# The last four on-chip transposes of a fused attention and feed-forward kernel go to the DMA, and the loads around them move

## The chip, the core and the metric

The kernel runs on one core of a Trainium2 chip. The metric is the device time of one execution, in microseconds (us): the median of several runs. The engines of the core are named as in the profile: PE (matrix engine; PEld is its weight load), DVE (vector), ACT (scalar), POOL and SP. POOL and SP also issue DMA transfers, each in the order of its own instruction stream.

## The reference

Batch 8, 8 heads, 1024 rows, head size 64. Keys and values are first projected along the rows to 64, then there is an ordinary softmax attention against these 64, and its output goes through a gated feed-forward block of width 1536:

```
k_proj = einsum('ks,bhsd->bhkd', E, k);  v_proj = einsum('ks,bhsd->bhkd', F, v)
scores = matmul(q, k_proj^T) / 8
attn   = exp(scores - max) / (sum + 1e-9)
x      = matmul(attn, v_proj), heads side by side: (8192, 512)
g = x @ w_gate;  out = (g * sigmoid(g) * (x @ w_val)) @ w_out
```

All inputs and the output are float32; the kernel computes in bf16 on PE.

## The kernel before, in words

The work is cut into 16 chunks of 512 rows: batch `b` (0 to 7) and half `ch` (0 or 1), chunk number `c = 2b + ch`. The feed-forward block is the main stream: for each chunk, 12 steps `f`, so 192 steps `t = 12c + f`. A step is four matmuls of 128x512 against `w_gate` (`f_g`, L322), four against `w_val` (`f_v`, L322), and, one chunk late, one or two groups of four against `w_out` (`f_y`, L360). Every third group of a chunk's `f_y` ends a 128-row output tile, which ACT copies out (`ysb`, L370) and SP stores (L372).

The attention of the next batch is written by hand into the gaps of this stream. Slot `2t` lies after `f_g` of step `t`, slot `2t+1` after its `f_v` and `f_y`; `put(slot, function, ...)` places a piece there, and every engine executes its share in this order (nothing is reordered later). In each slot the loads come first. The pieces, with the names used below:

- `load_k`, `load_v`, `load_q`, `load_wo`: DMA transfers issued by POOL, with a cast to bf16. k and v are 1 MB each in bf16 and per batch, a half of q 0.5 MB (one per chunk), a half of the output weights 0.75 MB. At the start of the kernel they are listed one after the other, beside the gate and value weights.
- KV (`u_KV`, L147): the two projections, 8 matmuls each for k and v. KT (`u_KT`, L172): the projected keys turned over and written as the block-diagonal tile `BD`.
- The turn of q, either on PE, T (`u_T`, four pieces per chunk with four transposes each, L193, and a copy by ACT), or by one DMA transpose, TD (`u_TD`, tile `qTd`, L205, issued by SP).
- S (`u_S`, L227): the scores, eight pieces per batch, `u` = 0 to 7 (0 to 3 belong to the first half), four small matmuls each, and the exponential on ACT (`ee`). R (`u_R`): sum and reciprocal on DVE. N (`u_N`, L258): the product of both on POOL, tile `AAd` (or `AA`).
- The turn of the attention weights, either on PE, A (`u_A`, four pieces per chunk with four transposes each, L274, and a copy by DVE), or by one DMA transpose, AD (`u_AD`, tile `AT`, L212, issued by SP). SP's stores of output tiles and its TD and AD stand in one stream.
- PV (`u_PV`, L285): the product with the values, four pieces per chunk, from `AT` to the chunk's input `xT`.

The list `BY_DMA` says which chunks are turned by DMA: before, all of batches 1 to 7 but the first half of batch 1. Batch 0 is always turned on PE. In `place(b)` stand the slots of a batch: `sa` for S, `sp` for PV, and, for batch 1, `tt` and `ta` for T and A. For b of 3 and more, S lies in slots `48(b-1)+6` and every third after it; these are the same before and after.

Of the kernel before, what the change touches and what calls it, by code (L numbers as in the profile page):

```python
# [15 lines left out]
B = 8  # L16
# [11 lines left out]
CH = 2  # L28
CW = 512
NIT = B * CH * NFT  # L30
BY_DMA = [(b, ch) for b in range(1, B) for ch in range(CH)][1:]


@with_exitstack
def kernel(
# [49 lines left out]
    def load_k(b, h0=0, h1=H):  # L85
        if h0 == 0:
            kb[b] = kv_pool.tile([P, H, NJ, D], BF16, name="kb", tag="kb")
        nc.gpsimd.dma_start(
            out=kb[b][:, h0:h1].rearrange("p h j d -> p h (j d)"),
            in_=k[b, h0:h1].rearrange("h (p j) d -> p h (j d)", j=NJ),  # L90
        )
# [10 lines left out]
    def load_q(b, ch, parts=1):  # L102
        t = q_pool.tile([P, H, 4, D], BF16, name="qb", tag="qb")
        qb[b, ch] = t
        n = H // parts
        for i in range(parts):
            nc.gpsimd.dma_start(
                out=t[:, i * n : (i + 1) * n].rearrange("p h j d -> p h (j d)"),
                in_=q[b, i * n : (i + 1) * n].rearrange("h (p c j) d -> p c h (j d)", c=2, j=4)[:, ch],
            )  # L110

    def load_w_gv(c0, c1, which=(0, 1)):
        cs = slice(c0 * P, c1 * P)
        for wsrc, wdst in [((moe_w_gate, wg), (moe_w_val, wv))[i] for i in which]:
            nc.gpsimd.dma_start(
                out=wdst[:, :, cs],
                in_=wsrc[:, cs].rearrange("(t p) c -> p t c", p=P),
            )

    def load_wo(i):  # L120
        nc.gpsimd.dma_start(
            out=wo[:, 6 * i : 6 * (i + 1), :],
            in_=moe_w_out[6 * i * P : 6 * (i + 1) * P, :].rearrange("(t p) c -> p t c", p=P),
        )
# [93 lines left out]
    def u_S(b, u, at="a"):  # L218
        ch, w = divmod(u, 4)
        g, i = divmod(w, 2)  # L220
        ps = bank(at, [P, 4, P], FP32, "sc")
        if (b, ch) in BY_DMA:
            t = qT[b, ch, "d"][:].rearrange("p (h i) t -> p i h t", i=2)[:, i, 4 * g : 4 * g + 4]
# [163 lines left out]
    def put(s, fn, *a):  # L387
        slots[s].append((fn, a))

    def place(b):  # L390
        s0 = 48 * (b - 1)
        if b == 1:
            put(30, u_TD, 1, 1)
            put(34, u_KV, 1, "k")
            put(36, u_KT, 1)
            put(40, u_KV, 1, "v")
            sa = (37, 38, 39, 40, 48, 50, 52, 54)
            tt = (35, 36, 37, 38)
            ta = (41, 42, 43, 44)
            put(57, u_AD, 1, 1)  # L400
            sp = (43, 44, 45, 46, 66, 67, 68, 69)
        else:
            put(s0, u_KV, b)
            put(s0 + 3, u_KT, b)
            o = 14 if b == 2 else 6
            put(s0 + (3 if b == 2 else -6), u_TD, b, 0)
            put(s0 + (5 if b == 2 else -4), u_TD, b, 1)
            sa = [s0 + o + 3 * j for j in range(NJ)]
            put(sa[3] + 4, u_AD, b, 0)
            put(sa[7] + 4, u_AD, b, 1)  # L410
            sp = [s0 + i for i in (39, 41, 43, 45, 57, 59, 61, 63)]
        for j in range(NJ):
            if (b, j // 4) not in BY_DMA:
                put(tt[j], u_T, b, j)
                put(ta[j], u_A, b, j)
            put(sa[j], u_S, b, j)
            put(sa[j] + 1, u_R, b, j)
            put(sa[j] + 1, u_N, b, j)
        for i in range(8):
            put(sp[i], u_PV, b, i // 4, i % 4)  # L420
# [5 lines left out]
    with tc.manual_schedule():  # L426
        load_k(0, 0, 4)
        ef = []
        for which, src in (("E", E), ("F", F)):
            raw = const.tile([KP, S], FP32, name=f"{which}raw")  # L430
            nc.sync.dma_start(out=raw[:], in_=src)
            ef.append(raw)
        zeros = const.tile([P, CW], BF16, name="zeros")
        nc.vector.memset(zeros[:], 0.0)
        make_identity(nc, ident_fp[:])
        make_identity(nc, ident_bf[:])
        for i in range(2):
            nc.vector.memset(BD[i][:], 0.0)
            nc.vector.memset(BDV[i][:], 0.0)

        def turn(which):
            for half in range(2):
                ps = bank("v", [P, 4, KP], FP32, "efp")
                for i in range(4):
                    j = 4 * half + i
                    nc.tensor.transpose(
                        out=ps[:, i, :],
                        in_=ef[which][:, bass.ds(j, P, step=NJ)],
                        identity=ident_fp[:KP, :KP],
                    )  # L450
                js = slice(4 * half, 4 * half + 4)
                copy((nc.scalar, nc.vector)[which], (ET, FT)[which][:, js, :], ps[:])

        def warm(n):

            ps = bank("v", [P, CW], FP32, "warm")
            for _ in range(n):
                nc.tensor.matmul(  # L458
                    out=ps[:], lhsT=zeros[:, 0:P], rhs=zeros[:],
                    start=True, stop=True,  # L460
                )


        load_k(0, 4, 8)
        load_q(0, 0, 2)
        load_v(0, (0, 4, 8))
        load_w_gv(0, 1)
        load_w_gv(1, 2)
        load_w_gv(2, 4)
        warm(8)  # L470
        turn(0)
        turn(1)
        warm(7)
        u_KV(0, "k", (0, 4), at="y")
        warm(2)
        u_KT(0, at="v", prs=(0, 2))
        warm(2)
        u_KV(0, "k", (4, 8), at="y")
        warm(2)
        u_KT(0, at="v", prs=(2, 4))  # L480
        u_T(0, 0, "a", nc.scalar)
        u_T(0, 1, "a", nc.vector)
        u_T(0, 2, "a", nc.scalar)
        u_S(0, 0, "g")
        u_T(0, 3, "v", nc.vector)
        u_S(0, 2, "g")
        u_S(0, 1, "a")
        u_S(0, 3, "a")
        u_R(0, 0)
        u_N(0, 0)  # L490
        u_R(0, 2)
        u_N(0, 2)
        load_w_gv(4, 6, (0,))
        u_KV(0, "v", (0, 4), at="y")
        warm(1)
        u_A(0, 0, nc.scalar)
        u_R(0, 1)
        u_N(0, 1)
        u_R(0, 3)
        u_N(0, 3)  # L500
        u_A(0, 2, nc.scalar)
        u_KV(0, "v", (4, 8), at="y")
        load_w_gv(4, 6, (1,))
        load_q(0, 1)
        load_w_gv(6, 8)
        load_w_gv(8, 10)
        load_w_gv(10, 12)
        load_wo(0)
        load_wo(1)
        load_k(1)  # L510
        warm(1)
        u_PV2(0, 0, 0, 0, nc.scalar)
        u_PV2(0, 0, 1, 0, nc.vector)
        u_A(0, 1, nc.scalar)
        u_A(0, 3, nc.vector)
        f_mm(0, 0, 0, 0)
        f_mm(0, 0, 1, 0)
        u_PV2(0, 0, 0, 1, nc.scalar)
        u_PV2(0, 0, 1, 1, nc.vector)
        f_mm(0, 1, 0, 0)  # L520
        f_mm(0, 1, 1, 0)

        for i, u in enumerate(range(4, 8)):
            put(12 + i, u_T, 0, u)
            put(14 + i, u_S, 0, u)
            put(15 + i, u_R, 0, u)
            put(15 + i, u_N, 0, u)
            put(19 + i, u_A, 0, u, nc.scalar)
        put(21, u_PV, 0, 1, 0)
        put(22, u_PV, 0, 1, 1)  # L530
        put(23, u_PV, 0, 1, 2)
        put(23, u_PV, 0, 1, 3)
        put(20, load_q, 1, 0)
        put(20, load_v, 1)
        put(20, load_q, 1, 1)
        for b in range(1, B):
            place(b)
        for b in range(2, B):
            s0 = 48 * (b - 1) - (12 if b == 2 else 24)
            put(s0, load_k, b)  # L540
            put(s0 + 2, load_v, b)
            put(s0 + 4, load_q, b, 0)
            put(s0 + 6, load_q, b, 1)

        for s in slots:
            slots[s].sort(key=lambda x: x[0] not in (load_k, load_v, load_q))


        ypart = defaultdict(list)
        for c in range(B * CH - 1):  # L550
            for n in range(NFT):
                f = n if c else 4 + (2 * n + 1) // 3
                ypart[(c + 1) * NFT + f].append((c, n))

        for t in range(NIT):
            c, f = divmod(t, NFT)
            i = 1 if t < 2 else None
            f_g(c, f, i)
            run_slot(2 * t)
            f_v(c, f, i)  # L560
            for a in ypart.pop(t, ()):
                f_y(*a)
            run_slot(2 * t + 1)
        for n in range(9):
            f_y(B * CH - 1, n)
        f_y_last(B * CH - 1, 3)
        assert not slots and not ypart
# [29 lines left out]
```

The softmax here doesn't subtract the row's maximum and nothing guards it: scores larger than these inputs give would overflow.

## Time and profile before

| | |
|---|---|
| median of 6 runs | 573.81 us (573.4 to 574.19) |
| time of the profiled execution | 573.73 us |
| its span in the profile | 572.0 us |
| PE busy | 562.4 us, 98% |
| DVE, ACT, POOL busy | 336.7, 236.9, 107.9 us |
| DMA, mean over the span | 107 GB/s |
| granted PE clock | 0.9 of full speed or more in every slice |

The profile times start at the beginning of the span; the 1.73 us between span and time lie around it. Rates of DMA count bytes as they are written, so a load with a cast counts at half of what is read.

### The profile page before, as it was taken

To read this page: it belongs to the slowest core of one execution; us is meant where nothing else is said; L and a number is where in the kernel's file an instruction comes from. 1 tells how busy PE (TensorE), PEld (TensorE's weight loads), DVE (VectorE), ACT (ScalarE), POOL (GpSimd) and SP (SyncE) were. 2 spreads that over 40 slices of the span, in tenths; PEclk is the share of its full clock that TensorE was granted. 3 is DMA by queue.
4 is the path that set the end of the run, shared out by engine and by line. 5 is a ranking of instruction groups with operands and counts; after the bars stand their busy time and mean duration, and the time that the engine had idled before them with its cause. 6 is when DMAs were issued, how large, how long until landed. Compare 5 with 4: busy or idle time off the path is not lost.

```text
span 572.0 us, 7867 instructions
## 1 busy us (share of the span) xinstructions
PE 562.4 (98%) x2910; PEld 268.5 (47%) x2967; DVE 336.7 (59%) x580; ACT 236.9 (41%) x416; POOL 107.9 (19%) x121
## 2 busy tenths in 40 slices
PE   8999999999999999999999999999999999999997
PEld 4654444444444444444444444444444444444444
DVE  2787566666466754666556665567546675554550
ACT  1665444354435434444335434354342543443232
POOL 6724121134002500124001330023200220000000
PEclk9999999999999999999999999999999999999999
DMA  9999993549901697038941499204990124100012
GB/s 168 195 201 206 201 154 76 91 71 195 202 32 46 109 192 153 18 75 128 192 103 38 63 177 198 59 20 92 188 182 36 43 51 74 38 37 27 30 39 92
DMA packets 105927, 61.34 MB, mean 107 GB/s; under 512 B 58016, under 2 KB 97696, under 8 KB 105888
## 3 DMA queue, kind: packets, MB, share of 16 engines
q0 software_dynamic: 42288, 29.89, 36.0%
q1 hardware_dynamic: 63312, 30.68, 25.3%
q8 instruction: 23, 0.38, 0.3%
q10 hardware_dynamic: 288, 0.26, 0.1%
q14 instruction: 16, 0.13, 0.1%
HBM read 60.29 MB, written 16.78 MB: 135 GB/s over the span
## 4 chain that ended last, share of the span: by engine, by line
PE 96%; ACT 1%; DMA 1%; issue 1%; DVE 1%; SPq 0%
PE yps L360 29%; PE vps L322 29%; PE gps L322 29%; PE kvp L147 3%; PE sc L227 3%; PE pv L285 2%; DMA Fraw<-in_F_dram 1%; PE warm L458 1%; PE aTp L274 0%; PE qTp L193 0%; PE kTp L172 0%; ACT xT L135 0%; DVE zz L242 0%; ACT th L334 0%; DVE AA L258 0%
## 5 line engine op out<-in xcount | busy, mean ns | idle before, releaser
L341 DVE SCALAR_TENSOR_TENSOR s<-th,gps 128x512 f32<-128x512 f32 x192 | 130.5, 680 | 138.0 <-ACT th L334 137.8
L322 PE MATMUL gps<-xT,wg 128*128 128x512 bf16 (+1 forms) x755 | 195.7, 377 | 1.2
L322 PE MATMUL vps<-xT,wv 128*128 128x512 bf16 (+1 forms) x761 | 195.9, 377 | 0.8
L360 PE MATMUL yps<-wo,hT 128*128 128x512 bf16 (+2 forms) x761 | 191.5, 376 | 0.8
L334 ACT ACTIVATE th<-gps 128x512 f32<-128x512 f32 x192 | 114.7, 597 | 162.6 <-PE gps L322 155.1
L346 DVE TENSOR_TENSOR hT<-s,vps 128x512 bf16<-128x512 f32 x192 | 132.0, 688 | 22.1 <-PE vps L322 1.5
L360 PEld LDWEIGHTS <-hT 128*128 128x128 bf16 x780 | 76.2, 98 | 89.9
L258 POOL TENSOR_TENSOR AAd<-ee,rr 128x512 bf16<-128x512 f32 x52 | 54.1, 1040 | 319.5 <-issue 168.5
L322 PEld LDWEIGHTS <-wv 128*128 128x128 bf16 x776 | 73.9, 98 | 82.9 <-issue 3.3
L322 PEld LDWEIGHTS <-wg 128*128 128x128 bf16 x776 | 74.0, 98 | 81.3 <-issue 0.6
L370 ACT ACTIVATE ysb<-yps 128x512 f32<-128x512 f32 (+1 forms) x65 | 38.4, 591 | 78.1 <-PE yps L360 74.4
L135 ACT CAST xT<-pv 128x512 bf16<-128x512 f32 x62 | 36.1, 585 | 51.3 <-PE pv L285 50.3
L242 DVE TENSOR_REDUCE zz<-ee 128x8 f32<-128x512 f32 x64 | 43.5, 679 | 17.7 <-ACT ee L231 17.6
L231 ACT ACTIVATE ee<-sc 128x512 f32<-128x512 f32 x64 | 37.8, 595 | 17.4 <-PE sc L227 17.4
L285 PE MATMUL pv<-AT,BDV 128*128 128x512 bf16 x60 | 22.6, 379 | 0.1
L227 PEld LDWEIGHTS <-qTd 128*128 128x128 bf16 x208 | 16.0, 98 | 12.3
L227 PE MATMUL sc<-BD,qTd 128*128 128x128 bf16 x208 | 20.1, 219 | 0.1
L135 DVE CAST BDV<-kvp 64x256 bf16<-64x256 f32 x14 | 6.0, 426 | 22.1 <-ACT ks L157 19.1
L258 POOL TENSOR_TENSOR AA<-ee,rr 128x512 bf16<-128x512 f32 x10 | 10.3, 1038 | 35.9 <-DVE rr L244 33.7
L244 DVE RECIPROCAL rr<-zz 128x8 f32<-128x8 f32 x64 | 13.0, 203 | 6.2
L147 PE MATMUL kvp<-kb,ET 128*64 128x512 bf16 (+1 forms) x72 | 15.5, 358 | 0.0
L147 PE MATMUL kvp<-vb,FT 128*64 128x512 bf16 (+1 forms) x72 | 15.5, 358 | 0.0
(49 smaller groups left out, 146.0 us busy)
## 6 DMA issues: line engine op xcount, KB each, us to landing
out_dram<-ysb SPq DMA_DIRECT2D x63, 256.0 KB, 2.3
qb<-in_q_dram POOLq DMA_DIRECT2D x15, 512.0 KB, 17.4
kb<-in_k_dram POOLq DMA_DIRECT2D x7, 1024.0 KB, 11.8
vb<-in_v_dram POOLq DMA_DIRECT2D x7, 1024.0 KB, 14.1
wo<-in_moe_w_out_dram POOLq DMA_DIRECT2D x2, 768.0 KB, 15.0
wg<-in_moe_w_gate_dram POOLq DMA_DIRECT2D x5, 256.0 KB, 10.1
wv<-in_moe_w_val_dram POOLq DMA_DIRECT2D x5, 256.0 KB, 10.4
kb<-in_k_dram POOLq DMA_DIRECT2D x2, 512.0 KB, 8.0
```

Source lines behind the costliest of these rows:

```text
L135: (nc.scalar.copy if eng is nc.scalar else eng.tensor_copy)(out=out, in_=in_)
L147: nc.tensor.matmul(out=t[lo : lo + 64, h0:h1].rearrange("p h d -> p (h d)"), lhsT=w[:, j, :], rhs=src[b][:, h0:h1, j, :], start=(j == 0), ...
L227: nc.tensor.matmul(out=ps[:, n, :], lhsT=t[:, n, :], rhs=BD[b % 2][:, 4 * g + n, :], start=True, stop=True)
L231: nc.scalar.activation(out=e[:].rearrange("p h j k -> p (h j k)"), in_=ps[:].rearrange("p a k -> p (a k)"), func=AF.Exp, scale=scale,)
L242: nc.vector.reduce_sum(out=z[:], in_=e[:], axis=AX.X)
L258: eng.tensor_tensor(out=a.rearrange("p j h k -> p h j k"), in0=ee.pop((b, u))[:], in1=rr.pop((b, u))[:].unsqueeze(3).to_broadcast([P, 4, 2 ...
L322: nc.tensor.matmul(out=ps[:, ts], lhsT=(wg, wv)[w][:, kt, f * P : (f + 1) * P], rhs=x[:, kt, ts], start=(kt == 0), stop=(kt == NKT - 1),)
L334: nc.scalar.activation(out=th[:], in_=ps[:], func=AF.Tanh, scale=0.5)
L341: nc.vector.scalar_tensor_tensor(out=s1[:], in0=th[:], scalar=1.0, in1=g[:], op0=ALU.add, op1=ALU.mult)
L346: nc.vector.tensor_tensor(out=hT[c][:, f, :], in0=s1[:], in1=ps[:], op=ALU.mult)
L360: nc.tensor.matmul(out=yy[c][:, cs], lhsT=hT[c][:, f, i * P : (i + 1) * P], rhs=wo[:, f, cs], start=(f == 0), stop=(f == NFT - 1),)
L370: nc.scalar.activation(out=ysb[:, cs], in_=yy[c][:, cs], func=AF.Copy, scale=0.5)
```

## The change

- `BY_DMA` takes in the first half of batch 1. Its four T and four A pieces on PE go; a TD in slot 22 and an AD in slot 41 are added. The second half's TD moves from slot 30 to 39, its AD from 57 to 50.
- At the start, the first half of q of batch 1 is loaded (it was in slot 20), and k of batch 1 comes ahead of the output weights instead of behind them.
- Batch 1: KV of the keys moves from slot 34 to 29, KT from 36 to 32, S from (37 to 40, 48, 50, 52, 54) to (35 to 38, 43, 44, 45, 47), PV of the first half from 43 to 46 to 44, 45, 46, 46.
- Batch 2: its loads move from slots 36, 38, 40, 42 to 46, 47, 48, 48; KV from slot 48 to 58, KT from 51 to 61, TD from 51 and 53 to 60 and 62, S from 62 and every third to 65 and every third, AD from 75 and 87 to 78 and 90. PV stays (slots 87 to 93 and 105 to 111).

```diff
-BY_DMA = [(b, ch) for b in range(1, B) for ch in range(CH)][1:]
+BY_DMA = [(b, ch) for b in range(1, B) for ch in range(CH)]
...
         if b == 1:
-            put(30, u_TD, 1, 1)
-            put(34, u_KV, 1, "k")
-            put(36, u_KT, 1)
+            put(22, u_TD, 1, 0)
+            put(29, u_KV, 1, "k")
+            put(32, u_KT, 1)
             put(40, u_KV, 1, "v")
-            sa = (37, 38, 39, 40, 48, 50, 52, 54)
-            tt = (35, 36, 37, 38)
-            ta = (41, 42, 43, 44)
-            put(57, u_AD, 1, 1)
-            sp = (43, 44, 45, 46, 66, 67, 68, 69)
+            sa = (35, 36, 37, 38, 43, 44, 45, 47)
+            put(41, u_AD, 1, 0)
+            put(39, u_TD, 1, 1)
+            put(50, u_AD, 1, 1)
+            sp = (44, 45, 46, 46, 66, 67, 68, 69)
         else:
-            put(s0, u_KV, b)
-            put(s0 + 3, u_KT, b)
-            o = 14 if b == 2 else 6
-            put(s0 + (3 if b == 2 else -6), u_TD, b, 0)
-            put(s0 + (5 if b == 2 else -4), u_TD, b, 1)
+            put(s0 + (10 if b == 2 else 0), u_KV, b)
+            put(s0 + (13 if b == 2 else 3), u_KT, b)
+            o = 17 if b == 2 else 6
+            put(s0 + (12 if b == 2 else -6), u_TD, b, 0)
+            put(s0 + (14 if b == 2 else -4), u_TD, b, 1)
             sa = [s0 + o + 3 * j for j in range(NJ)]
             put(sa[3] + 4, u_AD, b, 0)
             put(sa[7] + 4, u_AD, b, 1)
             sp = [s0 + i for i in (39, 41, 43, 45, 57, 59, 61, 63)]
         for j in range(NJ):
-            if (b, j // 4) not in BY_DMA:
-                put(tt[j], u_T, b, j)
-                put(ta[j], u_A, b, j)
...
         load_w_gv(10, 12)
+        load_q(1, 0)
+        load_k(1)
         load_wo(0)
         load_wo(1)
-        load_k(1)
...
-        put(20, load_q, 1, 0)
         put(20, load_v, 1)
         put(20, load_q, 1, 1)
...
         for b in range(2, B):
-            s0 = 48 * (b - 1) - (12 if b == 2 else 24)
-            put(s0, load_k, b)
-            put(s0 + 2, load_v, b)
-            put(s0 + 4, load_q, b, 0)
-            put(s0 + 6, load_q, b, 1)
+            s0 = 48 * (b - 1) - 24
+            at = (46, 47, 48, 48) if b == 2 else (s0, s0 + 2, s0 + 4, s0 + 6)
+            put(at[0], load_k, b)
+            put(at[1], load_v, b)
+            put(at[2], load_q, b, 0)
+            put(at[3], load_q, b, 1)
```

## The prediction

> **What bounds the kernel now.** First the page: the engines' busy time and the chain that ended last.
>
> ```profile
> span 572.0 us, 7867 instructions
> PE 562.4 (98%) x2910; PEld 268.5 (47%) x2967; DVE 336.7 (59%) x580; ACT 236.9 (41%) x416; POOL 107.9 (19%) x121
> PE 96%; ACT 1%; DMA 1%; issue 1%; DVE 1%; SPq 0%
> ```
>
> PE is never free. The list of PE's waits has six entries, all before 21 us; the longest two:
>
> ```profile
> PE warm L458 <- DVE zeros L434: 1.2, 1, 1.2
> PE efp L446 <- DMA Fraw<-in_F_dram: 0.7, 1, 0.7
> ```
>
> So PE work taken out is won in full, and a wait put into PE's stream is lost in full: no other engine gives anything back. The question is only whether each moved piece still finds its data. A price for PE work comes from the starts in PE's timeline (its durations overlap):
>
> ```profile
> 66.00 0.39 PE L227 MATMUL sc<-BD,qT 128*128 128x128 bf16 x4
> 66.22 0.39 PE L193 MATMUL qTp<-ident_bf,qb 128*128 128x128 bf16 x4
> 66.45 0.38 PE L322 MATMUL gps<-xT,wg 128*128 128x512 bf16 x1
> ```
>
> Four transposes, or one S piece, cost 0.22 us; four matmuls of 128x512 cost 0.865 (f_g of t=29 from 102.71 to 103.57, its f_v to 104.44); KV of both 1.95 (87.67 to 89.62), KT 0.32.
>
> **What is removed.** Four T and four A, 8 x 0.22 = 1.76 us of PE. Their copies on ACT (4 x 0.5) and DVE (4 x 0.42) were hidden and bring nothing. KV, KT, S and PV are only moved: nothing. With no new wait: 573.73 - 1.76 = 572.0.
>
> The Trainium skill speaks against such a trade: "VectorE: DVE Perf Modes", Rules for kernel authors, would keep a 128x128 transpose on TensorE where PSUM is a fit target, and its table, The three transpose paths, gives 390 ns for one. At that figure the 32 removed would be worth 12.5 us by estimate and the sum below would end near 567. The rows above show 0.055 us each in this stream.
>
> **The start.** Landings before: last gate/value weight 38.5, output weights 42.2 and 46.6, k 51.6, first q half 54.3, v 59.3, second q half 62.0; so 2.7 us per half q, 5.0 per MB, 4.4 per half of the output weights, back to back. In the new order: q half 41.2, k 46.2, output weights 50.6 and 55.0, then v 60, q 62.7. TD in slot 22 starts at 41.2 among them. The TD at 62.01 among loads took 13.0 us to land; a load stream falls from 0.20 to 0.16 MB/us beside it, about 3 us lost. That makes k 47, output weights 52 and 57, v 63, q 66. Needed: k in slot 29 at 52.9, output weights at 58.6 and 61.6 (56.4 and 59 in their old place, plus the KV and KT put ahead of them), S in slot 35 at 62.9 (TD landed by 54.3), v at 70.7. Covered by 4 us or more: nothing. POOL has one more load to issue (0.9 us) before its next N, where it waited 6.85 us: nothing.
>
> **Batch 1.** SP gets past the store of slot 39 at 71.2. TD takes SP 1.7 to 3.5 us (87.79, 98.64) and lands after 4.4 to 5.4: 76.6, S needs it at 77.9. AD follows at 73 to 75, lands 4.3 to 5.4 later, 77.6 to 80.2; PV in slot 44 comes at 79.2. A wait of 0 to 1; I take 0.1.
>
> **First wait: v of batch 2, KV in slot 58.** Slot 58 is the end of f_g(29): 103.57 in the old trace, where KV and KT of batch 2 and all of T and A lay ahead: 103.57 - 1.95 - 0.32 - 1.76 = 99.5. The loads of batch 2 used to be queued at 47 to 49 us, 38 us early. Now k stands on POOL behind the N of the second S of slots 43 and 44. That S starts at 79.0: between its start and slot 58 lie 22 groups at 0.865 and 7 small pieces (S, PV) at 0.22, 20.6 together. How long from S to a load behind its N? POOL and PE at batch 3:
>
> ```profile
> 117.62 0.39 PE L227 MATMUL sc<-BD,qTd 128*128 128x128 bf16 x4
> 120.76 1.04 POOL L258 TENSOR_TENSOR AAd<-ee,rr 128x512 bf16<-128x512 f32 x1 [3.96 <-DVE rr L244]
> 121.74 0.94 POOL L88 DMA_DIRECT2D kb<-in_k_dram  x1
> 125.83 0.94 POOL L97 DMA_DIRECT2D vb<-in_v_dram  x1
> ```
>
> It was 4.1; here two R (1.03 each) share DVE with s and hT, so 4.1 to 4.8: k is issued at 83.1 to 83.8, I take 83.7, and v at 85.7, behind the next N. When does v land? The landing times of batch 3, by issue:
>
> ```profile
> kb<-in_k_dram POOLq DMA_DIRECT2D x1, 1024.0 KB, 11.8
> vb<-in_v_dram POOLq DMA_DIRECT2D x1, 1024.0 KB, 14.5
> AT<-AAd SPq DMA_TRANSPOSE x1, 17.4
> ```
>
> v landed 18.6 us after k was issued; batches 4 to 7 give 18.0 to 18.9. In all of them one AD and stores were in the queues, as here: AD of slot 50 at 89.5, 5.8 us behind k (4.2 at batch 3, 9 later). One sees the sharing in the queues' row for 134 to 135 us:
>
> ```profile
> q0 software_dynamic: 154, 0.16, 92.4%
> q1 hardware_dynamic: 153, 0.04, 29.6%
> ```
>
> Loads (q0) and transpose (q1) alternate packet for packet, 1 KB against 256 B. Batch 3 less 0.5 for the later AD: v at 83.7 + 18.1 = 101.8. PE waits 2.3 us. Ends: counted from v's own issue (13.2 to 14.5) it lands at 98.9 to 100.2, a wait of 0 to 0.7; with 18.9 from k, 3.1. I take 2.3, since k's bytes, not v's issue, fill the queue then. Behind it TD of slot 60 waits for q at about 106.8 and lands 5.0 to 6.5 later, S of slot 65 comes at 113.5: 0 to 0.5, I take 0.
>
> **Second wait: AD of batch 2, first half, PV in slot 87.** PV stays, AD moves three slots on. Before:
>
> ```profile
> 125.90 8.48 SPq L212 DMA_TRANSPOSE AT<-AAd  x1
> 134.48 5.48 SPq L372 DMA_DIRECT2D out_dram<-ysb  x2
> 144.21 0.38 PE L285 MATMUL pv<-AT,BDV 128*128 128x512 bf16 x1
> ```
>
> It landed at 125.90 + 17.4 = 143.3, 0.9 us ahead of PV. The loads of batch 3 (slots 72 to 78) stay, so it still runs against them. In this old time scale it now lies on SP behind the store of slot 77 (f_y done 130.6, copied and issued 131.45; before, that store had to wait for AD): issue 131.9. Its nearest rows are the AD of batches 4 to 7, issued 9 us behind k and just behind a store: 15.6 to 16.6. So 131.9 + 15.6 = 147.5, against PV at 144.21 + 0.22 (one more S ahead). PE waits 3.1. I take the low row, since the loads of batch 3 run out 1 us sooner after this issue than those of batches 4 to 7 do after theirs. Ends: a further 0.9 off for that, 2.2; with 16.6, 4.1.
>
> The Trainium skill, "Advanced Engine Details and Errata", X-Bar Transpose (TRN2), says that transposes by DMA are as fast as ordinary transfers, 350 to 400 GB/s; by that AD's 0.5 MB would take some 1.5 us by estimate, this wait would not exist, and the sum below would end at 574.4. Alone an AD landed in 4.3 us here, among loads in 15.6 to 17.4; I use the rows.
>
> From batch 3 on nothing changes; the slots have at least 8 us in hand there (TD at 148.28 landed at 154.8, S at 164).
>
> **Sum.** -1.76 + 0.1 + 2.3 + 3.1 = +3.7: 573.73 + 3.7 = 577.4 for a profiled execution. The median stands 0.08 above it: 577.5.
>
> **Rivals.**
> - Only AD is late (v's landing goes with its own issue): -1.76 + 3.1 + 0.4 = +1.7, 575.5. For it: v is queued 2 us behind k, not 4. Against it: at batch 3 the queue was never empty between them.
> - Only v is late: AD at 131.9 lands by 144.4, that is within 12.5 us: -1.76 + 2.3 = +0.5, 574.3. Against it: no AD among loads was under 15.6 (the one at 142.33, with the loads nearly done, took 8.8).
> - Faster: loads and transposes hinder each other less than in the rows of batch 3. The point of decision is 15.8 us from k's issue to v's landing, and 12.5 for AD. Alone, half a q landed 6.6 us after issue (79.25), so 2 MB would take 6.6 + 1.5 x 5.0 = 14.1 with nothing beside them. Then both waits vanish: 572.0.
> - Longer: also TD of slot 60 or AD of slot 41 late by 1 to 1.5: 578.5 or more.
> - That the first half of batch 1 is not turned in time by DMA (the change failing at its own aim) has 8 us against it.
>
> **How the numbers follow.** Both waits 0.60 (574.5 to 578.5 by their ends); only AD 0.13; only v 0.09; none 0.11; longer 0.07. The range 573.8 to 579.0 leaves out the faster case, part of "only v" and the tail of the last, under 0.2. A measurement of this kernel tells 0.2%, 1.15 us, from no change: 572.66 to 574.96. Faster 0.12; within 0.16 (most of "only v", a third of "only AD", the low end of both); slower 0.72.
>
> **What would show it.** PE busy down by 1.8; two new entries in PE's waits, kvp on vb near 100 us with about 2.3, pv on AT near 146 with about 3.1. Wrong, if PE has no wait after 21 us (then 572), if one of the two is missing, or if waits stand at the output weights near 58 or at k near 53.

## The result, and the profile after

The changed kernel takes 576.52 us in the middle (575.02 to 579.21, 19 runs), the kernel before 573.76 (39 runs). The ratio is 1.0054, 95% interval 1.0045 to 1.0063: slower by half a per cent, where 577.5 was forecast. The profiled execution took 577.42 us with a span of 575.6, so it lies 0.9 above the median. (What left PE are four T and four A pieces, 32 transposes; those of batch 0, 32 of each kind, still run on PE after the change, so the moved ones are not the last on the chip.)

The page of the changed kernel, the same lines as before:

```profile
span 575.6 us, 7803 instructions
PE 562.6 (98%) x2879; PEld 267.4 (46%) x2935; DVE 335.2 (58%) x576; ACT 234.8 (41%) x412; POOL 107.9 (19%) x121
PE 90%; DMA 5%; ACT 1%; DVE 1%; issue 1%; POOL 0%; DVEq 0%; ACTq 0%; POOLq 0%
```

The chain that ended last was 96% PE before and 1% DMA; now it is 90% PE and 5% DMA. (PE busy has not fallen by the 1.8 us that the forecast asked for, though PEld shows the 32 instructions gone, 2967 to 2935. Behind the start of this execution, see below, it did fall, by 1.2 us; the start shows 1.4 more for the same 290 matmuls, which ran in part at half pace. Starts and gaps are the better measure.) PE's waits, the two longest:

```profile
PE pv L285 <- DMA AT<-AAd: 2.3, 1, 2.3
PE kvp L147 <- DMA vb<-in_v_dram: 1.2, 1, 1.2
```

Both stand where they were expected, and behind the start there is no other new one. In PE's timeline, with the idle time and its releaser in brackets:

```profile
99.87 1.03 PE L322 MATMUL gps<-xT,wg 128*128 128x512 bf16 x4
100.83 0.40 PE L147 MATMUL kvp<-kb,ET 128*64 128x512 bf16 x1
102.45 0.38 PE L147 MATMUL kvp<-vb,FT 128*64 128x512 bf16 x1 [1.22 <-DMA vb<-in_v_dram]
...
144.39 1.03 PE L360 MATMUL yps<-wo,hT 128*128 128x512 bf16 x4
147.72 0.39 PE L285 MATMUL pv<-AT,BDV 128*128 128x512 bf16 x1 [2.31 <-DMA AT<-AAd]
```

KV works on k and v in pairs that start together (87.77 both in the trace before). Here the first matmul with k runs at 100.83 and the first with v 1.62 later: 1.6 us lost (the bracket counts less, since the modelled end of the k matmul lies inside). The group of f_y at 144.39 lasts 0.865, so PV could start at 145.26 and starts at 147.72: 2.46 lost.

The span can now be accounted for. Up to f_g of t=12 this execution is 1.23 us late (48.51 against 47.28), though up to there both kernels give PE the same work. PE's first projection shows why, before and after:

```profile
10.50 1.06 PE L147 MATMUL kvp<-kb,ET 128*64 128x256 bf16 x8
```

```profile
10.64 1.92 PE L147 MATMUL kvp<-kb,ET 128*64 128x256 bf16 x8
```

These are the same eight matmuls at nearly half the pace: in this execution PE came to its full pace later. (The granted clock reads 1.00 over this stretch, so why is not shown.) It belongs to the execution and not to the change: two further profiles of the changed kernel ran them in 1.06 and 1.03 us, from 8.61 and 9.69 on, and POOL issues the same loads in the same order in both kernels up to the last gate and value weights (near 27 us). So +1.23 (start) - 1.76 (transposes gone) + 1.6 + 2.5 = +3.6, the 3.6 between the spans.

### The profile page after: what moved, and what is told of

It reads as the page before. It is cut to its first block, busy times and chain, and to the rows that moved or that the text cites. A ratio compares the mean times of both kernels' runs of the same rounds, so it can differ in the third digit from the quotient of the medians.

```text
span 575.6 us, 7803 instructions
## 1 busy us (share of the span) xinstructions
PE 562.6 (98%) x2879; PEld 267.4 (46%) x2935; DVE 335.2 (58%) x576; ACT 234.8 (41%) x412; POOL 107.9 (19%) x121
## 4 chain that ended last, share of the span: by engine, by line
PE 90%; DMA 5%; ACT 1%; DVE 1%; issue 1%; POOL 0%; DVEq 0%; ACTq 0%; POOLq 0%
PE vps L322 27%; PE yps L360 27%; PE gps L322 26%; PE kvp L147 3%; DMA vb<-in_v_dram 3%; DMA AT<-AAd 3%; PE sc L227 2%; PE pv L285 2%; PE warm L455 1%; DVE zz L242 0%; PE kTp L172 0%; ACT xT L135 0%; POOL AAd L258 0%; PE efp L443 0%; PE aTp L274 0%
## 5 line engine op out<-in xcount | busy, mean ns | idle before, releaser
L258 POOL TENSOR_TENSOR AAd<-ee,rr 128x512 bf16<-128x512 f32 x56 | 58.2, 1041 | 347.7 <-issue 166.1
L227 PEld LDWEIGHTS <-qTd 128*128 128x128 bf16 x224 | 17.2, 98 | 13.2
L227 PE MATMUL sc<-BD,qTd 128*128 128x128 bf16 x224 | 21.6, 219 | 0.1
L147 PE MATMUL kvp<-kb,ET 128*64 128x512 bf16 (+1 forms) x72 | 16.6, 375 | 0.0
L107 POOL DMA_DIRECT2D qb<-in_q_dram x17 | 15.1, 889 | 0.0
## 6 DMA issues: line engine op xcount, KB each, us to landing
qb<-in_q_dram POOLq DMA_DIRECT2D x15, 512.0 KB, 18.1
```

The lines of the kernel that those rows point to most:

```text
L147: nc.tensor.matmul(out=t[lo : lo + 64, h0:h1].rearrange("p h d -> p (h d)"), lhsT=w[:, j, :], rhs=src[b][:, h0:h1, j, :], start=(j == 0), ...
L227: nc.tensor.matmul(out=ps[:, n, :], lhsT=t[:, n, :], rhs=BD[b % 2][:, 4 * g + n, :], start=True, stop=True)
L258: eng.tensor_tensor(out=a.rearrange("p j h k -> p h j k"), in0=ee.pop((b, u))[:], in1=rr.pop((b, u))[:].unsqueeze(3).to_broadcast([P, 4, 2 ...
```

## The experiments

Two theories stood against each other. The first is the forecast's: the 32 transposes are worth 1.76 us, and two waits on DMA cost 1.6 and 2.5. The rival: the DMA queues are over-full in this stretch, the two waits are where that shows by chance, and taken away they come back elsewhere. All experiments start from the changed kernel; times are medians, ratios stand against the kernel before in the same session (573.4 to 573.9 from one session to the next).

**The wait on v.** The loads of batch 2 one N earlier on POOL:

```diff
-            at = (46, 47, 48, 48) if b == 2 else ...
+            at = (45, 46, 47, 48) if b == 2 else ...
```

> The loads of batch 2 start one N earlier on POOL (slots 45 to 48). Theory of the two waits: k is issued some 2 us sooner after its S (82.6 instead of 84.8 in the trace of the changed kernel), v lands near 100.5, the 1.6 us of PE at KV of slot 58 go, the wait of PV on AT (2.5) stays: 576.5 - 1.6 = 574.9. Rival, the DMA is simply over-full there: the wait reappears at another piece of batch 2 (S of slot 65 on qTd, or PV on AT), 576.5 stays. Rival, lost clock: if the wait on v is what makes PE's clock drop in some executions, those vanish too and the spread of the times shrinks.

Measured 574.82 us, ratio 1.0020 (1.0008 to 1.0032), 1.7 under the changed kernel. Counted from its S, k was issued 2 us earlier, no wait of kvp is left in the list, and the other wait stayed where and what it was:

```profile
PE pv L285 <- DMA AT<-AAd: 2.6, 1, 2.6
```

So this wait was its own cost and did not move on. The spread of the times hardly shrank (573.74 to 577.57, against 575.02 to 579.21), and 6 of the 12 executions still have a mean granted clock under 0.998, so the third case of the expectation is not borne out.

**The wait on AT.** PV of batch 2, first half, two slots later:

```diff
-            sp = [s0 + i for i in (39, 41, 43, 45, 57, 59, 61, 63)]
+            sp = [s0 + i for i in ((41, 43, 45, 46) if b == 2 else (39, 41, 43, 45)) + (57, 59, 61, 63)]
```

> PV of batch 2, first half, in slots 89, 91, 93, 94 instead of 87, 89, 91, 93. Theory of the two waits: two slots are 2.6 us of PE work, so AT has landed (147.65 against PV at 145.25 + 2.6 = 147.85), the wait of 2.5 us goes, the 1.6 us on v stay: 576.5 - 2.5 = 574.0. Rival: AT is late for a reason that follows PV (the N or the store before it): the wait moves along, 576.5. Rival, lost clock: if this longer wait makes the clock drop, no run has a mean clock under 1.0 and the gain is over 2.5.

Measured 573.87 us, ratio 0.9998 (0.9989 to 1.0006), 2.65 under the changed kernel. PV on AT is gone from PE's waits; kvp on v stays with 1.4 at slot 58. AT landed 14.9 us after its issue, as before (15.0); only PE came later. Five of these 12 executions have such a lower clock too, so this wait is not what brings it about there either.

**Both.**

> Both edits. Theory of the two waits: no PE wait after 25 us, what is left is the 1.76 us of the 32 transposes: 573.8 - 1.8 = 572.0, faster than the kernel before by 0.3%. Rival, the transposes taken off PE were worth nothing, or cost comes back elsewhere: 573.8 or more.

Measured 572.29 us, ratio 0.9969 (0.9959 to 0.9980): faster than the kernel before by 1.6 us, and the fastest version here. No PE wait on a DMA is left but one in the first 10 us:

```profile
PE efp L443 <- DMA Fraw<-in_F_dram: 0.9, 1, 0.9
```

The gains are 1.70 and 2.65 singly and 4.23 together: the two costs add. The rival, that they come back elsewhere, falls.

**What the transposes are worth.** The kernel with both edits, and 32 transposes more on PE that nobody reads:

```diff
+            for i, x in enumerate((24, 25, 26, 27, 28, 30, 31, 33)):
+                put(x, u_idle_turn, 1, 0, i % 2)   # four nc.tensor.transpose of qb into a PSUM bank
```

> Starts from the kernel with both waits taken out (572.3) and puts 32 transposes back on PE, in eight groups of four in slots 24 to 33, whose result nobody reads. Theory: PE's work sets the time, so 8 x 0.22 = 1.76 us: 572.3 + 1.8 = 574.1, as the kernel before. Rival, what the change won came from the copies on ACT and DVE or from other waits: 572.3 stays.

Measured 573.82 us, ratio 1.0003 (0.9994 to 1.0012): 1.5 us more than with both edits, or 2.0 when each is counted from the kernel before in its own session (+0.37 and -1.63). That lies around the 1.76 expected, and level with the kernel before. No copies came back with them, so PE work alone accounts for the gain.

**Why AT is late: contention.** Only the loads of batch 3 move, ten slots later:

```diff
+            if b == 3:
+                at = tuple(x + 10 for x in at)
```

> Only the loads of batch 3 move, from slots 72 to 78 to 82 to 88; AD of batch 2 (slot 78) then runs without loads beside it. Theory, contention: AT lands 4.3 to 5.5 us after its issue instead of 15.0, PV does not wait; KV of batch 3 in slot 96 may get a wait of 0 to 2 on v. 576.5 - 2.5 + (0 to 2) = 574.0 to 576.0. Rival, AD is late by its place on SP behind the store, or the transpose is slow by itself: it still takes 10 us or more, and the wait on AT stays near 2.5.

Measured 574.28 us, ratio 1.0008 (0.9998 to 1.0018). The same AD, at the same place in SP's stream behind the same store, as the list of DMA issues has it (microseconds to landing last), changed kernel first, then with the loads out of the way:

```profile
AT<-AAd SPq DMA_TRANSPOSE x1, 15.0
```

```profile
AT<-AAd SPq DMA_TRANSPOSE x1, 4.4
```

The loads make 4.4 into 15.0. PV did not wait, and KV of batch 3 got no wait either (the 1.2 us on v at slot 58 stayed).

**Why it is late: its place.** AD three slots later:

```diff
-            put(sa[3] + 4, u_AD, b, 0)
+            put(sa[3] + (7 if b == 2 else 4), u_AD, b, 0)
```

> Starts from the changed kernel; only AD of batch 2, first half, moves from slot 78 to 81. Its wait at PV should grow by the 3.7 us of PE work in three slots, less what AD lands faster because the loads of batch 3 run out sooner (some 0.4 per us): from 2.5 to 4.5 to 6.2, 576.5 + 2.0 to 3.7 = 578.5 to 580.2. Question of the clock: if a PE wait of this length makes the granted clock drop, the profile shows a slice under full clock behind it and the time grows by a further 1 to 3 us; if it does not, no slice after 30 us is under full clock and the lower clock of some executions belongs to the start alone.

Measured 577.64 us, ratio 1.0068 (1.0048 to 1.0087). This was a miss: the wait did not grow (1.7 in the profile). SP's stream is the same with the AD in slot 78 or 81, because no store lies between; a slot does not tie an AD to PE's time, it only orders it on SP, where it runs once the store ahead of it is through and its N is done. So it is a repetition of the changed kernel and no test. The move that does change SP's order is this one, two slots back, ahead of the store of slot 77:

```diff
-            put(sa[3] + 4, u_AD, b, 0)
+            put(sa[3] + (2 if b == 2 else 4), u_AD, b, 0)
```

> Starts from the changed kernel; AD of batch 2, first half, goes from slot 78 to 76, which puts it ahead of the store of slot 77 in SP's stream (a move from 78 to 81 had changed nothing, since no SP instruction lies between). It then waits for its N alone (done 131.3 in the trace of the changed kernel, where AD was issued at 132.65) and has no 256 KB of store in front of it in the queue, some 2 us among loads. If the place behind the store makes AT late: AT lands 2.5 to 3.5 us sooner, the wait of 2.5 us at PV shrinks to 0 to 0.3, 576.5 - 2.4 = 574.1. If the later N (S moved by three slots) makes it late: AT lands 1.3 sooner at most, the wait stays over 1.1, 575.2 or more.

Measured 574.38 us, ratio 1.0012 (1.0000 to 1.0023), 2.1 less than the changed kernel. SP's timeline, changed kernel:

```profile
132.23 0.33 SPq L372 DMA_DIRECT2D out_dram<-ysb  x1
132.65 6.55 SPq L212 DMA_TRANSPOSE AT<-AAd  x1
```

and with AD ahead of the store, with PE's PV below it:

```profile
129.96 6.15 SPq L212 DMA_TRANSPOSE AT<-AAd  x1
```

```profile
144.51 0.39 PE L285 MATMUL pv<-AT,BDV 128*128 128x512 bf16 x1 [0.44 <-DMA AT<-AAd]
```

Counted from the issue of k of batch 3 (122.56 and 121.22), AD goes out 1.35 us sooner and lands 0.5 faster (14.5 against 15.0). Neither of the two cases of the expectation met it exactly: AT landed 1.9 us sooner, most of it because the store no longer held AD back on SP. That the other 0.5 comes from the 256 KB no longer ahead in the queue is not shown, since landings of the unmoved AD differ by more (14.4 to 15.3). AD now goes out as soon as N is done (129.93), so what is left of the wait, 0.4, is no longer due to SP's order.

**The order of the loads at the start.** k of batch 1 back behind the output weights:

```diff
         load_q(1, 0)
-        load_k(1)
         load_wo(0)
         load_wo(1)
+        load_k(1)
```

> Starts from the changed kernel; at the start, k of batch 1 goes back behind the output weights (the first half of q stays ahead of both). By the landings of the changed kernel (k 47.7, output weights 52.8 and 55.9) k would land near 56 and KV of slot 29, at 54.2, would wait some 2 us: 576.5 + 2 = 578.5, with an entry kvp on kb in PE's waits and none on the output weights. Rival, the order at the start is idle: no new wait, 576.5.

Measured 582.28 us, ratio 1.0155 (1.0141 to 1.0169). The wait came, with 4.2 instead of 2 us, since k landed near 56 as expected but PE was due there at 52.0 and not at 54.2 as in the late-starting trace of the changed kernel. And something was added to it:

```profile
56.37 3.62 PE L147 MATMUL kvp<-kb,ET 128*64 128x512 bf16 x8 [4.18 <-DMA kb<-in_k_dram]
59.93 1.89 PE L322 MATMUL gps<-xT,wg 128*128 128x512 bf16 x4
61.61 1.27 PE L322 MATMUL vps<-xT,wv 128*128 128x512 bf16 x4
```

After the wait, KV takes 3.56 us to the next start where the changed kernel takes 1.85, f_g 1.68 instead of 0.865. In the table of stages (PE clock third from the end):

```profile
52.00:54.00 2.00, 0.20 (x1) 0.00 (x0) 1.38 (x2) 0.00 (x0) 0.00 (x0) 1.00 1.21 195
54.00:56.00 2.00, 0.00 (x0) 0.00 (x0) 0.00 (x0) 0.00 (x0) 0.00 (x0) 0.81 1.22 196
56.00:58.00 2.00, 1.63 (x4) 0.71 (x5) 0.00 (x0) 0.00 (x0) 0.00 (x0) 0.50 1.21 195
...
62.00:64.00 2.00, 2.00 (x13) 0.90 (x12) 1.38 (x3) 0.67 (x2) 0.00 (x0) 0.98 1.01 141
```

PE went idle at 52.1; its granted clock halved near 55.2 and was full again at 62.1. That costs 1.71 + 0.82 + 0.24 = 2.8 us on top of the wait. So the order in which the change loads at the start is needed for slot 29.

**The loads of batch 2 as early as they were.**

```diff
-            at = (46, 47, 48, 48) if b == 2 else ...
+            at = (36, 38, 40, 42) if b == 2 else ...
```

> Starts from the changed kernel; the loads of batch 2 go back to slots 36 to 42. Theory, contention: v and q are then issued near 70 to 75 us, beside TD (72.3) and AD (74.5) of batch 1, which land after 8 to 13 us instead of 4.5; the wait on v at slot 58 (1.6) goes, but S of slot 43 (79.1) waits on qTd 1 to 6 and PV of slot 44 on AT some 2 to 4 more: 576.5 - 1.6 + (3 to 10) = 578 to 585. Rival, early loads are simply better: no wait at slots 43 and 44, 574.9.

Measured 588.5 us, ratio 1.0256 (1.0233 to 1.0280), the slowest here, and 3.5 above the range expected:

```profile
PE sc L227 <- DMA qTd<-qb: 9.7, 1, 9.7
```

TD, issued at 71.44 beside the loads of v and q, landed after 16.6 us instead of 8 to 13:

```profile
qTd<-qb SPq DMA_TRANSPOSE x1, 16.6
```

S of slot 43 waited 9.7 for it instead of 1 to 6, and the granted clock was again at half, from 80.6 to 90.8. AD, issued behind it, landed after 11.0, just in time for the PV that had been held up with S. With the new turns in slots 39 and 41, these loads cannot lie there.

**The changed kernel, twice more,** for one open point: of its 19 executions, the 8 with a mean granted clock of 0.994 to 0.997 took 577.8 us in the middle, those of 0.999 and more 576.0, while in the kernel before and in the one with both edits the two groups lie within 0.4 us.

> The changed kernel as it is, for the place of the lower clock: in 8 of its 19 executions the mean granted clock was 0.994 to 0.997, and these took 577.8 us in the middle, the others 576.0. The kernel before has such executions too, without being longer. If the profile falls on a lower clock: a slice under full clock behind the wait of PV on AT (146 to 152 us) says that this wait sometimes costs clock besides its own length; a slice in the first 20 us alone says that it does not. With full clock the profile tells nothing on it; the two waits should then be 1.6 and 2.5 us again.

> The same kernel and the same question as the run before it: where the slices under full clock lie, if the profile falls on a lower clock.

They took 574.92 and 576.78 us, both at full clock, so they cannot answer the question; the list of waits has 1.7 and 2.6 on AT. What they do show is how much the wait on AT varies. With the profiled execution and the AD in slot 81 there are four traces of this order: AT landed 14.4, 14.4, 15.0 and 15.3 us after its issue, and PE lost 1.9, 1.9, 2.5 and 2.7 us to it.

On the clock: waits of 2.3 to 2.6 us on AT left it at 1.00 wherever a trace has them. One of these traces is of an execution with the lower mean (0.997, the loads of batch 2 one N earlier, wait 2.6): its clock was at 0.50 from 8 to 10 us and full from 11 us on, so there the lower mean belongs to the start. Waits of 4.2 and 9.7 halved the clock after 3.1 and 2.3 us of idling. The lower mean is also as frequent in the kernel before (15 of 31 executions of one session) as in the changed one (8 of 19). Why the changed kernel's executions with the lower mean are longer, and why its median moved 0.5 us more than the terms, stays open: a longer wait on AT that costs clock in some of them would fit, and so would their starts; neither is shown.

## Why the prediction was right, by its steps

| step | forecast | measured |
|---|---|---|
| T and A off PE | -1.76 | -1.6 (both waits out, against before); +1.5 to 2.0 (put back) |
| start, AD of slot 41 | 0, 0.1 | no new wait |
| S to the issue of k, batch 2 | 4.7 | 4.6 (80.21 to 84.81) |
| k issued to v landed | 18.1 | 17.65 |
| wait of KV, slot 58 | 2.3 | 1.6 (1.3 to 1.8 in the others); its removal 1.7 |
| AD, issue to landing | 15.6 | 15.0 (14.4 to 15.3 in the other traces of this order) |
| AD issued to PV due | 12.5 | 12.6 |
| wait of PV, slot 87 | 3.1 | 2.5 (1.9 to 2.7 in the others); its removal 2.65 |
| sum | +3.7 | -1.76 + 1.6 + 2.5 = +2.3; medians +2.76 |

Mechanism, place and sign were right for each. The two terms that were mis-sized are the waits, 0.6 to 0.7 too large each. Both are a difference of two long times, and in both the long one was the landing among loads: 18.1 against 17.65, 15.6 against 15.0. For v the range 18.0 to 18.9 of the later batches had been lowered by 0.5 for a later AD, and the true value lies lower still; the further 0.2 is in the issue and in PE's own time. For AD the lowest row was taken, with 0.9 less named as an end; 0.6 of it was real. Both times a row of later batches was taken nearly as it stood; that more traffic lies beside the transfers there is the likely reason for the excess, but no run tests it. That the profiled execution took 577.42, just what was forecast for one, is luck: its late start (1.23) made up for the waits that were too large.

The rival "the waits vanish, 572.0" is the kernel with both edits (572.29): it describes what the change could be with v 2 us sooner and PV two slots later. The premise that a wait is lost in full, and no more, held for these two; the waits of 4.2 and 9.7 in the experiments cost clock on top. The other price that the forecast named for the 32 transposes, 12.5 us, is far off: 1.5 to 2.0 were measured.

The forecast named a rule that denied the second wait, that a transpose by DMA is as fast as an ordinary transfer (the Trainium skill, "Advanced Engine Details and Errata", X-Bar Transpose (TRN2)). Alone AD landed in 4.4 us here, beside loads in 15.0, so the measurement decides against pricing a transpose by that rule where loads run beside it.

## What to carry to other kernels

Where one engine carries the whole span, a move off it pays its own time there (1.5 to 2.0 measured for 1.76), and each wait put in costs its length, or more than that when it is long enough to cost clock (2.8 us on top of 4.2): read the margin of every piece that moves, not the busy shares. A transfer's landing time belongs to its company: price it from rows with the same neighbours, and look in the trace for pieces that did not move but whose supplier did (PV stayed, AD moved behind a store). Here 1.6 us were won and 4.2 given back, and two edits of one and two slots brought them back.

## What the runs showed of the hardware that was not expected

- An idle stretch of PE costs more than its length once it is long enough: in the waits of 9.7 and 4.2 us the granted clock fell to 0.50 after 2.3 and 3.1 us of idling, and it took 2.7 and 5.7 us of work to come back. The Trainium skill, "TensorE: Matmul & The Clock Gate", Why this matters for your kernels, warns of idle gaps over some 3 us. Both gaps here were longer than that and agree, though in one the clock fell after 2.3 us already; waits of 2.3 to 2.6 us left the clock at 1.00 in the traces that have them.
- A DMA transpose of 512 KB took 4.4 us alone, 14.4 to 15.3 beside the loads of batch 3, and 16.6 beside those of v and q of batch 2.
- The start of the same kernel varies by some 2 us from one execution to another: in the three profiles of the changed kernel the first projection began at 8.61 to 10.64 us and took 1.03 to 1.92, and f_g of t=12 began at 46.38 to 48.51.
